# Attention into a SwiGLU block: when the pieces of V are loaded, and when one copy is queued

## Chip, core and metric

The kernel runs on one core of a Trainium2 chip. The metric is the device time of one execution in microseconds, of which several runs are given. An execution under the hardware profiler gives the trace that is read here. The engines are TensorE (PE; its weight loads are a row of their own, PEld), VectorE (DVE), ScalarE (ACT), GpSimd (POOL) and SyncE (SP), which issues most of the transfers.

## What is computed

For 8 batches of 8 heads, 576 positions and head dimension 64: causal attention whose scores get a bias from a running sum of max(s, 0), then a gated feed-forward block over all 4608 tokens.

```
scores = scale * q @ k.T;  cum = cumsum(max(s, 0))
scores = where(causal, -1e9, scores + min(-(cum_i - cum_j), 0))
attn = softmax(scores);  x = (attn @ v), heads side by side     # 4608 x 512
g = x @ w_gate;  out = (g * sigmoid(g) * (x @ w_val)) @ w_out
```

## The kernel before

**Attention.** The 64 pairs of batch and head are worked in 16 half-batches of 4 heads. In the code `h` is the half-batch, `step` its head (0 to 3) and `ci` one of the four pieces of a head's score matrix (`score_piece`, L352). Half-batches 2b and 2b+1 are batch b; I call h "even" or "odd". A score piece is one to four matmuls (L373) from the operand tile `kq` into a PSUM bank, and one ACT activation (L383) that takes the exponential and frees the bank. The weighted sum with V (`av_piece`, L410) is followed by a DVE reciprocal and multiplication (`av_out`, L426 and L427), which free its bank. There are 8 banks; `take` gives out the one that was freed longest ago.

**Feed-forward.** `ffn_items(tt)` yields the work of tile tt (512 tokens) in small items: for each of 12 column blocks a gate product G and a value product V (`gate_value`, matmuls at L643), then the output product (L700 for tiles 0 and 1, L749 after). A gate product is followed by ACT's tanh (`th`, L664) and DVE's `pp` (L666), which frees its bank; a value product by DVE's `ht` (L677). The products read `XT`, the transposed attention output, one 128-row part per matmul.

**The order** is written out by hand: after each feed-forward item the loop pumps `attn_items` up to a given position, and each score piece calls `side` (L481) and `side_v` (L531), which hold tables of what else is issued there. Every engine works through its own instructions in that order. SP has one queue; an SP instruction that waits holds up all that follow.

**How k and q come in.** For half-batch hb: `load_qk` brings both from memory (rawk, rawq, 576 KB each); a cast makes them bf16 (ck, cq); `scratch` (L272) writes them to memory (ks, qs, 288 KB each); `transposes` (L281) reads them back transposed into pk and pq, single buffers; `split` (L286) is four DVE copies from pk and pq to `kq`. I write "ks 8" or "pk 8" for those of half-batch 8. Splits are not issued at once: `side` puts them into the list `later`, and `do_later(1)` takes one out at fixed feed-forward items (in tile 1 after every second item), `do_later(4)` the rest before the next transposes and at the start of a half-batch.

**How V comes in.** V of batch bn is five pieces of up to 128 positions (256 KB, the last 128 KB), each a transfer of its own on SP (`load_v`, L156) into `rawv`, which is a single buffer, and a cast into `vt` (`cast_v`, L167) on ACT for batch 3 and later (L171). V of batch bn is loaded in half-batch 2(bn-1) and cast in 2(bn-1)+1: batch 3 in half-batches 4 and 5, batch 4 in 6 and 7. A cast waits for its own piece alone. I write "V 3 piece 2".

**How x goes out.** For each pair of heads from batch 2 on, POOL writes the output to memory (`x_out`, xs) and SP reads it back transposed into `XT` (`x_in`, L451, after odd steps), in one or two parts.

Of the kernel before, what the change touches and what calls it, by code (L numbers as in the profile page):

```python
# [19 lines left out]
def kernel(  # L20
# [11 lines left out]
    nc = tc.nc  # L32
    PSUM = bass.MemoryType.PSUM

    B, H, S, D = q.shape
# [68 lines left out]
    first = first_sbuf.enter_context(tc.tile_pool(name="first", bufs=1))  # L104
# [9 lines left out]
    with tc.manual_schedule():  # L114
# [37 lines left out]
        def load_qk(hb):  # L152
            load_one(hb, "k")
            load_one(hb, "q")

        def load_v(b, cs, eng=nc.sync):  # L156
            if 0 in cs:
                loaded["v", b] = raw.tile([128, NCH, H, D], FP32, tag="rawv", bufs=1, name="rawv")
            t = loaded["v", b]
            for c in cs:  # L160
                n = 128 if c < 4 else TAIL
                eng.dma_start(
                    t[0:n, c, :, :],
                    v[b, :, c * 128 : c * 128 + n, :].rearrange("h p d -> p h d"),
                )

        def cast_v(b, c, eng):  # L167
            n = 128 if c < 4 else TAIL
            dst, src_t = VT[b % 2][0:n, c, :, 0:D], loaded["v", b][0:n, c, :, :]
            if eng is nc.scalar:  # L170
                nc.scalar.copy(dst, src_t)  # L171
            else:
                eng.tensor_copy(dst, src_t)  # L173
# [9 lines left out]
        def aug(hb, engs, hhs=range(HB)):  # L183
            for hh in hhs:
                r, e = divmod(hh, 2)
                r0 = 64 * (1 - r)
                bh = hb * HB + hh
                engs[hh].dma_start(  # L188
                    KQ[hb % 2][r][r0 : r0 + 4, :, e * S : (e + 1) * S],
                    HL[bh : bh + 1, :, :, :],  # L190
                )
# [61 lines left out]
        def cast_one(hb, name, eng):  # L253
            cts[name, hb] = cp.tile([128, J, NR, D], BF16, tag="c" + name, bufs=2, name="c" + name)
            dst = cts[name, hb].rearrange("x j r d -> x r j d")
            src_t = loaded[name, hb]
            if eng is nc.scalar:
                nc.scalar.copy(dst, src_t)
            else:
                eng.tensor_copy(dst, src_t)  # L260
# [11 lines left out]
        def scratch(hb):  # L272
            for name, SC in (("k", KS), ("q", QS)):
                nc.sync.dma_start(
                    SC[hb].rearrange("(x j) c -> x (j c)", j=J),
                    cts[name, hb].rearrange("x j r d -> x (j r d)"),
                )
# [3 lines left out]
        def transposes(hb):  # L281
            for name, SC in (("k", KS), ("q", QS)):
                prs[name, hb] = cp.tile([128, NR * S], BF16, tag="p" + name, bufs=1, name="p" + name)
                nc.sync.dma_start_transpose(prs[name, hb], SC[hb])
# [186 lines left out]
        def do_later(n):  # L471
            while n > 0 and later:
                f, *args = later.pop(0)
                f(*args)
                n -= 1
# [5 lines left out]
        def side(h, step, ci):  # L481
            bh = HB * h + step
            for c in V1_AT.get((bh, ci), ()):
                cast_v(1, c, nc.gpsimd)
            if bh == H + 4 and ci == 3:
                load_v(2, range(5))
            if h == 4 and (step, ci) in ((0, 1), (2, 1)):
                load_qk(6 + step // 2)
            if h >= 5 and h + 3 < NHB and (step, ci) == (0, 1):
                load_qk(h + 3)  # L490
            hb = h + 1
            if NPE <= hb < NHB:
                late = hb == NPE
                if late and (step, ci) == (0, 1):
                    scratch(hb)
                if late and (step, ci) == (0, 3):
                    transposes(hb)
                if (step, ci) == (0, 1):
                    aug(hb, GP4)
                first = 1 if hb < NPE + 3 else 0  # L500
                if step in (first, first + 1) and ci == (3 if late else 1):
                    for r in range(NR):
                        later.append((split, hb, "kq"[step - first], r))
            hb = h + 2
            if hb == NPE and step == 3 and ci % 2 == 1:
                cast_one(hb, "kq"[ci // 2], nc.gpsimd)
            if NPE < hb < NHB:
                six = hb == NPE + 1
                if (step, ci) == ((2, 0) if six else (0, 2)):
                    cast_one(hb, "k", nc.scalar)  # L510
                if (step, ci) == ((2, 2) if six else (1, 2)):
                    cast_one(hb, "q", nc.scalar)
                if (step, ci) == ((3, 0) if six else (2, 0)):
                    scratch(hb)
                if (step, ci) == (3, 3 if six else 0):
                    do_later(NR * 2)
                    transposes(hb)
            if ci != 1:
                return
            bn = h // 2 + 1  # L520
            if 3 <= bn < B:
                if h % 2 == 0:
                    if step == 2:
                        load_v(bn, (0, 1))
                    if step == 3:
                        load_v(bn, (2, 3, 4))

        V2_AT = {(1, 0): 0, (1, 1): 1, (1, 2): 2, (1, 3): 3, (2, 0): 4}
        V_AT = {(1, 0): 0, (2, 0): 1, (2, 2): 2, (3, 0): 3, (3, 2): 4}

        def side_v(h, step, ci):  # L531
            bn = h // 2 + 1
            if h == 4 and (step, ci) in V2_AT:
                cast_v(2, V2_AT[step, ci], nc.gpsimd)
            if 3 <= bn < B and h % 2 == 1 and (step, ci) in V_AT:
                cast_v(bn, V_AT[step, ci], nc.scalar)

        seconds = []

# [21 lines left out]
        def attn_items():  # L561
            for kk in range(H, BH + 2):
                h, step = divmod(kk, HB)
                if kk < BH:
                    if step == 0:
                        do_later(NR * 2)
                    if step == 1 and 3 < h + 1 < NPE:
                        cast_one(h + 1, "k", nc.gpsimd)
                        cast_one(h + 1, "q", nc.gpsimd)
                    if step == 2 and 3 < h + 1 < NPE:  # L570
                        aug(h + 1, GP4)
                    for ci in range(4):
                        score_piece(kk, ci)
                        side(h, step, ci)
                        side_v(h, step, ci)
                        yield kk + 0.1 + ci / 8
                        if (step, ci) in PREP_AT.get(h, ()):
                            prep_one(
                                h + 1, PREP_AT[h][step, ci],
                                (nc.scalar, nc.vector)[ci // 2] if h == 2 else None,  # L580
                            )
                            yield kk + 0.1 + ci / 8
# [327 lines left out]
        def pick(side):  # L910
            b = PICK[side]
            for lo in range(2):
                for c0, c1 in ((0, 512), (512, S)):
                    nc.tensor.matmul(
                        banks[:, b + c0 // 512, 0 : c1 - c0], sel[:, lo, :],
                        HL[:, lo, 1, c0:c1], start=(lo == 0), stop=(lo == 1),
                        skip_group_check=True,
                    )

        def picked_row(side):  # L920
            b = PICK[side]
            src_t = banks.rearrange("p b n -> p (b n)")[up, b * 512 : b * 512 + S]
            dst = KQ[0][0][up, side, 0:S]
            if side == 1:
                nc.scalar.activation(
                    dst, src_t, AF.Identity, bias=r_m[up, 0:1], scale=r_k[up, 0:1]
                )
            else:
                nc.vector.tensor_scalar(
                    dst, src_t, r_q[up, :], r_k[up, :], ALU.mult, ALU.add  # L930
                )
            give(b)
            give(b + 1)
# [102 lines left out]
        at = attn_items()  # L1036
# [84 lines left out]
```

## Time and profile before

| | |
|---|---|
| runs | 374.61 us median, 373.37 to 375.18 (3 runs) |
| the profiled execution | 373.92 us; its span 371.97 us, so 1.95 us lie outside the span |
| clock granted to PE | 0.998 of full speed |
| busy | PE 363.2, DVE 291.1, ACT 239.9, POOL 212.4 us |
| moved by DMA | 64.21 MB, most of it on SP's queue (41.46 MB) |

"Busy" is the union of an engine's instructions. Matmuls overlap, and their ends are modelled: one of 512 columns is shown with 0.379 us, but in an unbroken row each starts 0.216 us after the one before (four in 0.86 us), one of 65 columns 0.029 us. So I count what PE loses from start to start. In a timeline row the bracket is the engine's idle time before it and what ended it. When a transfer has landed is read from the trace's record of semaphore updates: each transfer of this kernel's queues makes 16, and I take the last.

### The profile page before, as it was taken

How to read it: one execution, taken by the hardware profiler on the slowest of the kernel's cores; microseconds unless marked ns; L12 is line 12 of the kernel's file. 1: busy time of each engine (PE TensorE's matmuls, PEld its weight loads, DVE VectorE, ACT ScalarE, POOL GpSimd, SP SyncE). 2: the span in 40 equal slices, each digit the busy share in tenths (PEclk: the TensorE clock that was granted, in tenths of full speed). 3: DMA queues.
4: the chain of work that ended last, by engine and by line, in shares of the span. 5: the costliest groups of instructions: out<-in, count | busy, mean ns of one | idle time of the engine just before them, and what ended most of it. 6: DMA issues, size and time to landing. Idle time of an engine off the chain costs nothing.

```text
span 372.0 us, 8786 instructions
## 1 busy us (share of the span) xinstructions
PE 363.2 (98%) x3288; PEld 230.3 (62%) x3288; DVE 291.1 (78%) x585; ACT 239.9 (65%) x470; POOL 212.4 (57%) x325
## 2 busy tenths in 40 slices
PE   7899999999999999999999999999999999999996
PEld 6684556655555557855685558655865585476465
DVE  8978776377985899589967897699868867975984
ACT  8877776778886967688757875786565523323321
POOL 8983556955266547594749464955675516315320
PEclk9999999999999999999999999999999999999999
DMA  7999999799879996996789484994142113002003
GB/s 238 220 254 259 215 272 257 239 299 227 252 172 307 199 268 181 162 285 217 214 179 263 160 185 157 265 210 114 40 121 62 35 30 118 0 3 86 28 0 113
DMA packets 97133, 64.21 MB, mean 173 GB/s; under 512 B 77228, under 2 KB 82724, under 8 KB 97092
## 3 DMA queue, kind: packets, MB, share of 16 engines
q1 hardware_dynamic: 84964, 41.46, 46.9%
q0 software_dynamic: 12128, 22.21, 22.7%
q8 instruction: 25, 0.41, 0.5%
q14 instruction: 16, 0.13, 0.1%
HBM read 37.90 MB, written 19.86 MB: 155 GB/s over the span
## 4 chain that ended last, share of the span: by engine, by line
PE 83%; DVE 10%; DMA 2%; ACT 2%; issue 2%; POOL 1%; DVEq 0%; ACTq 0%
PE banks L643 43%; PE banks L749 17%; PE banks L373 9%; PE banks L410 7%; PE banks L700 5%; DVE kq L330 3%; DMA pk<-ks 2%; DVE pp L666 2%; DVE ht L677 1%; DVE kq L288 1%; ACT th L664 1%; POOL vt L173 1%; ACT pt L383 1%; PE banks L459 1%; PE banks L301 0%
## 5 line engine op out<-in xcount | busy, mean ns | idle before, releaser
L383 ACT ACTIVATE pt<-banks 128x512 bf16<-128x512 f32 (+1 forms) x256 | 120.4, 511 | 29.8 <-PE banks L373 17.1
L643 PE MATMUL banks<-XT,wg 128*128 128x512 bf16 x432 | 111.4, 379 | 0.4 <-DVE pp L666 0.3
L643 PE MATMUL banks<-XT,wv 128*128 128x512 bf16 x432 | 110.9, 379 | 0.1
L664 ACT ACTIVATE th<-banks 128x512 bf16<-128x512 f32 x108 | 64.7, 599 | 56.3 <-PE banks L643 51.4
L666 DVE SCALAR_TENSOR_TENSOR pp<-th,banks 128x512 bf16<-128x512 bf16 x108 | 73.7, 682 | 18.3 <-ACT th L664 18.0
L677 DVE SCALAR_TENSOR_TENSOR ht<-pp,banks 128x512 bf16<-128x512 bf16 x108 | 74.1, 687 | 10.3
L373 PE MATMUL banks<-kq 128*128 128x128 bf16 (+4 forms) x576 | 76.4, 240 | 0.8 <-DVE kq L330 0.3
L686 POOL TENSOR_TENSOR ht<-ht 128x512 bf16<-128x512 bf16 x35 | 40.4, 1154 | 53.3 <-DVE su L684 53.2
L373 PEld LDWEIGHTS <-kq 128*128 128x128 bf16 x576 | 46.1, 98 | 30.7 <-issue 2.4
L643 PEld LDWEIGHTS <-wv 128*128 128x128 bf16 x432 | 38.4, 98 | 36.2 <-issue 0.2
L643 PEld LDWEIGHTS <-wg 128*128 128x128 bf16 x432 | 38.4, 98 | 34.1 <-issue 0.7
L410 PEld LDWEIGHTS <-pt 128*128 128x128 bf16 x960 | 41.8, 98 | 17.7 <-issue 0.7
L388 POOL TENSOR_SCALAR_AFFINE_SELECT pt<-pt 128x512 bf16<-128x512 bf16 x56 | 36.6, 653 | 25.9 <-ACT pt L383 21.7
L410 PE MATMUL banks<-vt,pt 128*128 128x65 bf16 x960 | 46.8, 194 | 0.5 <-DVE ot L427 0.4
L444 POOL DMA_DIRECT2D xs<-ot x24 | 21.7, 904 | 30.4 <-DVE ot L427 28.0
L749 PEld LDWEIGHTS <-ht 128*128 128x128 bf16 x336 | 31.2, 98 | 4.3
L427 DVE TENSOR_TENSOR ot<-banks,rc 128x320 bf16<-128x320 f32 x64 | 31.5, 492 | 2.2
L188 POOL DMA_DIRECT2D kq<-HL x48 | 29.2, 610 | 0.0
L700 PE MATMUL banks<-wo,ht 128*128 128x512 bf16 x96 | 25.8, 379 | 0.0
L749 PEld LDWEIGHTS <-su 128*128 128x128 bf16 x252 | 23.6, 98 | 3.3
L814 POOL TENSOR_TENSOR ysb<-ysb 128x512 f32<-128x512 f32 x12 | 15.2, 1269 | 15.3 <-DVE ysb L808 15.3
L749 PE MATMUL banks<-WS,ht 128*128 128x256 bf16 x168 | 22.9, 273 | 0.0
(101 smaller groups left out, 377.2 us busy)
## 6 DMA issues: line engine op xcount, KB each, us to landing
out_dram<-ysb POOLq DMA_DIRECT2D x32, 256.0 KB, 4.0
rawv<-in_v_dram SPq DMA_DIRECT2D x28, 256.0 KB
rawk<-in_k_dram SPq DMA_DIRECT2D x12, 576.0 KB
rawq<-in_q_dram SPq DMA_DIRECT2D x12, 576.0 KB
xs<-ot POOLq DMA_DIRECT2D x24, 160.0 KB, 3.7
ks<-ck SPq DMA_DIRECT2D x11, 288.0 KB
qs<-cq SPq DMA_DIRECT2D x11, 288.0 KB
rawk<-in_k_dram POOLq DMA_DIRECT2D x3, 576.0 KB, 6.0
```

The source lines that it names most:

```text
L373: nc.tensor.matmul(sc[:, o : o + w], T[:, 1, e * S + 128 * tj : e * S + 128 * (tj + 1)], T[:, 0, e * S + lo : e * S + hi], start=not maske ...
L383: nc.scalar.activation(pt[:, c0 : c0 + n], sc, AF.Exp, scale=0.125)
L388: nc.gpsimd.affine_select(pt[:, 1088:1600], pt[:, 1088:1600], pattern=[[0, 4], [1, 128]], compare_op=ALU.is_ge, fill=zreg, base=0, channel ...
L410: nc.tensor.matmul(av[:, bi * (D + 1) : (bi + 1) * (D + 1)], pt[:, c0 : c0 + 128], VT[b % 2][:, tj, h, :], start=(tj == 0), stop=(tj == bi),)
L427: nc.vector.tensor_mul(ot[:, :, e * D : (e + 1) * D], av3[:, :, 0:D], rc[:, :, None].to_broadcast([128, NCH, D]),)
L643: nc.tensor.matmul(view(bs, TT), w[:, c, f0 : f0 + 128], xt[:, c, :], start=(c == 0), stop=(c == 3),)
L664: nc.scalar.activation(th, pg, AF.Tanh, scale=0.5)
L666: nc.vector.scalar_tensor_tensor(pp, in0=th, scalar=1.0, in1=pg, op0=ALU.add, op1=ALU.mult)
L677: nc.vector.scalar_tensor_tensor(hp[:, 2 * k2 : 2 * k2 + 2, :].rearrange("p a n -> p (a n)"), in0=pp, scalar=0.5, in1=pv, op0=ALU.mult, op ...
L686: (nc.vector if ft == NFT - 1 else nc.gpsimd).tensor_sub(hp[:, 1:3, :], hp[:, 1:4:2, :], hp[:, 0:3:2, :])
L700: nc.tensor.matmul(view(pys[ts_], DM), hps[ft // 2][:, 2 * (ft % 2) + half, c0 : c0 + 128], WO[j][:, ft % WKO, :], start=(ft == 0), stop=( ...
L749: nc.tensor.matmul(ps, lhs(p), rhs(p), start=(first and p == 0), stop=(last and p == NP - 1), skip_group_check=True,)
```

## The change

In `side` the loads of V get tables of their own, one piece at an entry. An entry is (0 for an even half-batch or 1 for an odd one, step, ci).

```
-                if step in (first, first + 1) and ci == (3 if late else 1):
+                if step in (first, first + 1) and ci == (3 if late and step == first else 1):
                     for r in range(NR):
                         later.append((split, hb, "kq"[step - first], r))
...
-            if ci != 1:
-                return
-            bn = h // 2 + 1
-            if 3 <= bn < B:
-                if h % 2 == 0:
-                    if step == 2:
-                        load_v(bn, (0, 1))
-                    if step == 3:
-                        load_v(bn, (2, 3, 4))
+            if h >= 4:
+                odd = h % 2
+                at = VLOAD_AT if h > 5 else V3LOAD_AT
+                if h // 2 + 1 < B and (odd, step, ci) in at:
+                    load_v(h // 2 + 1, (at[odd, step, ci],))
+
+        VLOAD_AT = {(0, 0, 3): 0, (0, 1, 0): 1, (1, 0, 0): 2, (1, 0, 3): 3, (1, 1, 0): 4}
+        V3LOAD_AT = {(0, 3, 3): 0, (1, 0, 0): 1, (1, 0, 3): 2, (1, 1, 0): 3, (1, 1, 2): 4}
...
+        V3_AT = {(1, 2): 0, (2, 0): 1, (2, 2): 2, (3, 0): 3, (3, 2): 4}
         V_AT = {(1, 0): 0, (2, 0): 1, (2, 2): 2, (3, 0): 3, (3, 2): 4}
...
+            at = V_AT if bn > 3 else V3_AT
-            if 3 <= bn < B and h % 2 == 1 and (step, ci) in V_AT:
-                cast_v(bn, V_AT[step, ci], nc.scalar)
+            if 3 <= bn < B and h % 2 == 1 and (step, ci) in at:
+                cast_v(bn, at[step, ci], nc.scalar)
```

Before, pieces 0 and 1 were issued at (even, step 2, ci 1) and pieces 2 to 4 at (even, step 3, ci 1). After it, for batch 4 and later, pieces 0 and 1 come at the beginning of the even half-batch and pieces 2 to 4 at the beginning of the odd one. For batch 3, piece 0 comes at the last score piece of half-batch 4, after the transposes of half-batch 6, and pieces 1 to 4 in half-batch 5; the cast of its piece 0 moves from (step 1, ci 0) to (step 1, ci 2). In half-batch 4 the copies of q 5 are put into `later` at (step 2, ci 1), before at (step 2, ci 3). No transfer, cast or copy is added or taken away.

## Prediction

> **What bounds the kernel now.** I read the busy totals first, then the busy time in stretches of 10 us, then the timeline where PE loses time.
>
> ```profile
> PE 363.2 (98%) x3288; PEld 230.3 (62%) x3288; DVE 291.1 (78%) x585; ACT 239.9 (65%) x470; POOL 212.4 (57%) x325
> ```
>
> PE sets the time. The stretches show 10.00 us of PE in every ten from 60 to 360 us except two, the first and the last here (the first number after the stretch is its length, then PE, PEld, DVE, ACT, POOL, each with its count).
>
> ```profile
> 80.00:90.00 10.00, 9.74 (x86) 5.52 (x84) 8.42 (x17) 7.58 (x16) 5.03 (x9) 1.00 0.99 267
> ...
> 130.00:140.00 10.00, 9.60 (x84) 5.29 (x82) 9.33 (x20) 7.01 (x16) 4.85 (x8) 1.00 0.89 260
> ```
>
> The change begins at half-batch 4 (67 us), so these two stalls are all it can win. The timeline has both.
>
> ```profile
> 82.25 0.95 DVE L288 COPY kq<-pq 64x1152 bf16<-64x1152 bf16 x1
> ...
> 83.34 0.38 PE L373 MATMUL banks<-kq 128*128 128x128 bf16 x4 [0.26 <-DVE kq L288]
> ```
>
> Stall 1: the matmuls before it are nine of 65 columns from 82.65; at 0.029 each their turn ends at 82.91; PE goes on at 83.34: 0.43 us, for the first copy of q 5.
>
> ```profile
> 125.62 0.84 DVE L288 COPY kq<-pk 64x1152 bf16<-64x1152 bf16 x1 [0.76 <-DMA pk<-ks]
> ...
> 130.01 1.03 PE L643 MATMUL banks<-XT,wg 128*128 128x512 bf16 x4
> ...
> 131.44 0.47 PE L410 MATMUL banks<-vt,pt 128*128 128x65 bf16 x10 [0.40 <-DVE ot L427]
> ```
>
> Stall 2: four matmuls from 130.01 at 0.216 end at 130.87; PE goes on at 131.44: 0.57 us. It waits for the multiplication of the head before (DVE, 130.90 to 131.39), and DVE has gone without a pause worth the name since 125.62, where it had stood 0.76 us for pk 8. So the ceiling of a gain is 0.43 + 0.57 = 1.00 us.
>
> **Copies of q 5: nothing.** Queued later or sooner, they leave `later` at its slots. In tile 1 these come after the value products, every second item: the first takes the first k copy (77.44), the next the second (79.30), the third the first q copy (82.25). By the loops, q entered the list at half-batch 4 step 2 ci 3, between the first slot and the second; ci 1 lies there too. The list gives the k copies first, so every copy keeps its place on DVE, and stall 1 stays. A gain would need an earlier slot; that is excluded. 0.00.
>
> **pk 8 sooner: -0.57.** Its chain on SP:
>
> ```profile
> 108.94 2.45 SPq L451 DMA_TRANSPOSE XT<-xs  x2
> 111.50 0.53 SPq L274 DMA_DIRECT2D ks<-ck  x1
> 112.12 0.38 SPq L274 DMA_DIRECT2D qs<-cq  x1
> 112.55 1.81 SPq L162 DMA_DIRECT2D rawv<-in_v_dram  x2
> 118.37 2.59 SPq L284 DMA_TRANSPOSE pk<-ks  x1
> ```
>
> ks 8 lands at 118.32, then the transpose is issued and lands 7.22 us later (125.59), behind V 4 pieces 0 and 1 (120.44, 121.74). pk 7 and pk 9, with no V between, took 4.05 and 4.15. The change puts the two pieces ahead of the x transposes (108.94) and of ks 8. They cost the queue 2 x 0.9 to 1.3 us (between the landings of pieces 0 and 1: V 3 0.92, V 4 1.30), say 2.3. Against that SP comes sooner to this place: k 9, the transfer ahead of it, was issued at 107.81, 5.26 us of transposes after ks 7 had landed (102.55). ks 7 can gain from nothing to 1.9 us (k 9 needs the x output that landed at 103.38, and two x transposes of 1.25 after it: 105.9); I take 0.7, nearer to nothing, since V 3 is now ahead of it. So ks 8 lands at 118.32 + 2.3 - 0.7 = 119.9 and pk 8 4.15 later, 124.1. DVE is ready for it at 125.62 - 0.76 = 124.86. The wait goes, and stall 2 with it: -0.57; ends -0.57 (nothing else waits there) and 0 (pk 8 lands at 125.6 again).
>
> **V 3 against its casts: +1.0.** Here something new may be late. Before, all of V 3 had landed at 91.24. Now SP goes: ks 6 directly behind q 7 (landed 83.54), landing about 84.3 where it was 86.42; pk 6 84.3, pq 6 85.6 (by their 1.18 and 1.42), piece 0 87.0, the x transposes 87.6 (2.55), piece 1 90.2, k 8 90.9, q 8 91.5, pieces 2, 3, 4 at 92.0, 92.6, 93.2. k 8 took 4.16 us to land, q 8 1.51 more: 95.1 and 96.6. A piece is 0.8 to 0.9 behind the one before: piece 2 at 97.4, 3 at 98.3, 4 at 98.8. The casts stand here (before, nothing waited):
>
> ```profile
> 95.45 0.64 ACT L171 CAST vt<-rawv 128x512 bf16<-128x512 f32 x1
> ...
> 96.37 0.60 ACT L664 ACTIVATE th<-banks 128x512 bf16<-128x512 f32 x1 [0.17 <-PE banks L643]
> ...
> 97.22 0.67 DVE L666 SCALAR_TENSOR_TENSOR pp<-th,banks 128x512 bf16<-128x512 bf16 x1
> ...
> 98.68 1.03 PE L643 MATMUL banks<-XT,wv 128*128 128x512 bf16 x4
> ```
>
> The first is the cast of piece 2. ACT works in order: behind a waiting cast stand the exponentials and this tanh, behind the tanh DVE's pp, which frees the bank that PE takes at 98.68. A delay d of the cast ends the tanh at 96.97 + d, pp 0.73 later at 97.70 + d; with 0.05 to hand over, PE stands d - 0.93. With d = 97.4 - 95.45 = 1.95: 1.0 us, which a full PE never gets back. Ends: 0 (piece 2 by 96.4) and 2.4 (two us later than I think: the slowest of a transfer's 16 updates came 1.7 after the others at q 7 and at ks 7). Pieces 0 (landing 91, cast now near 92.0) and 1 (94.1 against 93.50) cost nothing beyond that; 3 and 4 come in the shadow of 2. The 0.96 us that DVE stood for pk 6 at 92.67 go too, but PE lost nothing by them.
>
> All of this takes it that a transfer waits for those ahead of it on SP's queue: the 118 SP transfers issued from 60 to 262 us landed in the order of issue, every one.
>
> [...]
>
> **x of batch 2: 0.** The last matmul of tile 2's first gate product needs the x transpose issued at 108.94; it landed at 116.31 and was used at 117.05. The two V 4 pieces now go ahead: 116.31 + 2.3 - 0.7 = 117.9, and the need moves by the 1.0 above to 118.05. Ends 0 and 1.6 (SP no sooner, V 3 in time: 118.6 - 117.05).
>
> **Batch 4 on otherwise: 0.** After pk 8 (119.9), pq 8 (121.2) and one x transpose (122.6), SP issues V 4 piece 2 at 124.0, k 10 and q 10 at 124.6 and 125.2, pieces 3 and 4 by 126.4. Piece 2 lands 4 us later, 128, against its cast at 130.68; k 10 and q 10 by 130.8 (q 10 took 6.54 behind three pieces of V; 5.6 with one ahead), pieces 3 and 4 by 132.5, against 133.72 and 136.09. Later batches have more room: V 5's pieces 2 to 4 go out around k 12, which was issued at 163.89 after them and landed with q 12 by 170.88; without the pieces ahead of pk 10 (issue 2.28 and 2.72 us, else 1.2 and 1.4) that is some 3 us sooner, so they land by about 168, against casts at 170.30, 172.79 and 175.16. Pieces 0 and 1 fall where SP stood idle (142 to 149). PE loses nothing there now, so nothing can be won.
>
> **Sum.** -0.57 + 1.0 = +0.43 on 373.92 (span 371.97 + 1.95): 374.35. The median of the runs is 0.69 above the profiled execution: 375.0.
>
> **Rivals.** (a) Everything in time: pieces 2 and on land by 96.4, pk 8 by 124.9: -0.57, 374.0. For it: DMA moved 49 GB/s at 94, there is room; against it: 1.15 MB of k 8 and q 8 stand ahead. (b) The x transpose is the late one, V 3 in time: +1.6, stall 2 gone in its shade, since DVE's work moves with PE: net +1.1, 375.7. (c) Slower, on the side I don't forecast: the queue of V 3 at the casts. From a landing of piece 2 at 98.9 (d = 3.45, 2.5 - 0.57 = +1.9) the loss is over 0.5%; at 99.4 it is 3.0 - 0.57 = +2.4, 377.0. For it: 7 to 8 us from issue to landing happened here (V 3 before, 7.4 and 7.9); against it: those stood behind k 7, q 7 and two output stores at once, and this stretch has no stores. (d) The change doesn't do what it says: true of the q 5 copies, by the list; that is in the forecast.
>
> **Chances.** Forecast 0.45, (a) 0.27, (b) 0.10, (c) 0.15, something else gaining over 0.5% 0.03. 0.5% (1.87 us) is about what a measurement of this kernel tells from no change. Faster 0.03, slower 0.17, the rest 0.80. Range: from (a) less 0.6 for the spread of the runs, 373.4, to 376.7, between (b) and (c).
>
> **What would show it.** Stall 1 as before, 0.43; no DVE wait for pk 8 or pk 6; pk 8 landing near 124; an ACT wait of 1 to 2 us before the cast of V 3 piece 2 and a PE stall near 99. If ACT does not wait there, (a) holds; if PE stands at tile 2's first gate product, (b); if stall 1 goes, my reading of the list is wrong.

## The result, and the profile after

| | before | after |
|---|---|---|
| median of 6 runs each, side by side | 374.26 us (373.35 to 375.66) | 379.37 us (376.77 to 380.99) |
| the profiled execution, its span | 373.92 us, 371.97 | 379.21 us, 377.3 |

The ratio of the means is 1.0127, with a 95% interval of 1.0082 to 1.0172. The change costs 1.3%, about 5 us, and lies above the predicted range. Below, the times are medians of all executions, while a ratio leaves out an execution that is more than 1.5% above the fastest of its kernel (one each of e1_v3_only, e2_v4_only and e8_v4_four_ahead). (In the changed file the lines behind the tables are one higher: L643 is L644, L664 is L665, L666 is L667; in some of the experiments L643 is L645 or L647.)

Where PE loses it is told first by its waits. The view gives the line, what it waited for, the total, how often, and the longest.

```profile
PE banks L644 <- DMA XT<-xs: 2.0, 1, 2.0
PE banks L644 <- DVE pp L667: 1.4, 2, 1.0
PE banks L373 <- ACT pt L383: 0.7, 1, 0.7
PE banks L373 <- DVE kq L288: 0.3, 1, 0.3
```

The first three lines have no large counterpart in the kernel before; the last is stall 1, unchanged. The stretches of 10 us (length, then PE, PEld, DVE, ACT, POOL, the granted clock, the DMA share, GB/s) place them:

```profile
80.00:90.00 10.00, 9.74 (x85) 5.53 (x84) 8.42 (x17) 7.31 (x15) 5.04 (x9) 1.00 0.78 184
90.00:100.00 10.00, 9.00 (x80) 4.96 (x78) 6.51 (x13) 6.87 (x15) 2.68 (x5) 1.00 0.86 236
100.00:110.00 10.00, 9.30 (x86) 5.34 (x86) 9.62 (x19) 9.01 (x18) 6.51 (x11) 1.00 0.72 162
110.00:120.00 10.00, 9.23 (x81) 5.06 (x79) 6.17 (x12) 6.18 (x13) 5.00 (x10) 1.00 1.13 253
120.00:130.00 10.00, 8.76 (x63) 4.48 (x63) 5.69 (x13) 5.08 (x10) 4.68 (x8) 0.83 1.03 245
130.00:140.00 10.00, 10.00 (x85) 5.51 (x84) 9.13 (x18) 8.95 (x18) 4.92 (x7) 1.00 0.79 208
```

80 to 90 is as before. 130 to 140 is full now: stall 2 has gone. From 90 to 130 PE loses in two places, and from 120 to 130 the clock column has 0.83: a part of it (122.48 to 125.90 us) ran at half clock, 0.50. The timeline of PE at these places:

```profile
83.33 0.38 PE L373 MATMUL banks<-kq 128*128 128x128 bf16 x4 [0.26 <-DVE kq L288]
...
99.49 0.19 PE L373 MATMUL banks<-kq 128*128 128x64 bf16 x1 [0.68 <-ACT pt L383]
100.70 1.02 PE L644 MATMUL banks<-XT,wv 128*128 128x512 bf16 x4 [1.02 <-DVE pp L667]
...
121.24 0.38 PE L644 MATMUL banks<-XT,wg 128*128 128x512 bf16 x1 [2.01 <-DMA XT<-xs]
...
123.12 1.91 PE L644 MATMUL banks<-XT,wg 128*128 128x512 bf16 x4
```

Counted from start to start, PE loses 0.85 + 1.18 = 2.03 us at 99 to 101 and 2.17 us before 121.24. The last row is no wait: four matmuls of 512 columns, 1.03 us elsewhere, take 1.91 at half clock.

**The first loss** comes from ACT, which stands for a piece of V 3:

```profile
94.48 1.08 ACT L383 ACTIVATE pt<-banks 128x512 bf16<-128x512 f32 x2
98.70 0.62 ACT L171 CAST vt<-rawv 128x512 bf16<-128x512 f32 x1 [3.13 <-DMA rawv<-in_v_dram]
...
99.34 0.59 ACT L665 ACTIVATE th<-banks 128x512 bf16<-128x512 f32 x1
```

That is the cast of piece 2, which stood at 95.45 before. Behind it are the exponentials that PE's first wait names, and the tanh that must come before the pp of the second. **The second loss** is tile 2's first gate product, waiting for the x transpose of pair 11 (the last pair of heads of batch 2). Before, its four matmuls ran without a wait:

```profile
116.41 1.02 PE L643 MATMUL banks<-XT,wg 128*128 128x512 bf16 x4
```

Both losses go back to SP's queue (start, time in issue; after the change):

```profile
90.34 0.47 SPq L145 DMA_DIRECT2D rawq<-in_q_dram  x1
90.86 6.96 SPq L162 DMA_DIRECT2D rawv<-in_v_dram  x3
97.98 2.46 SPq L451 DMA_TRANSPOSE XT<-xs  x2
...
109.97 0.57 SPq L145 DMA_DIRECT2D rawk<-in_k_dram  x1
110.59 0.47 SPq L145 DMA_DIRECT2D rawq<-in_q_dram  x1
111.11 1.29 SPq L162 DMA_DIRECT2D rawv<-in_v_dram  x2
112.50 5.68 SPq L451 DMA_TRANSPOSE XT<-xs  x2
```

k 8 landed at 94.26 and q 8 only at 97.79, 7.44 us after its issue; V 3's pieces 2, 3 and 4 followed at 98.67, 100.01 and 100.31. The issue of piece 4 alone held SP from 92.89 to 97.82, until q 8 was in. The x transposes behind it wait for an output of x that POOL writes, issued at 90.60; it took 7.36 us to land (97.96), where before it took 3.42. So two things kept these transposes until 97.98: the held issue and this write. So all that follows on SP is late, k 9 among it: issued at 109.97, landed at 114.50, where before it was 107.81 and 112.35. Behind k 9 now stand q 9 and V 4's pieces 0 and 1 (landed 117.84 and 120.03), and then pair 11's x transpose, 121.20, where it was 116.31.

The sum for this execution: 2.03 + 2.17 + 1.7 (3.41 us at half clock) - 0.57 (stall 2) = 5.33, against 377.3 - 371.97 = 5.3 in span. Two later profiles of the same kernel have the first loss again, but half of the second and no half clock behind it (next section), so this sum is not that of every execution.

### The profile page after: what moved, and what is told of

It reads as the page before. It is cut to its first block, busy times and chain, and to the rows that moved or that the text cites. A ratio compares the mean times of both kernels' runs of the same rounds, so it can differ in the third digit from the quotient of the medians.

```text
span 377.3 us, 8795 instructions
## 1 busy us (share of the span) xinstructions
PE 365.5 (97%) x3288; PEld 231.4 (61%) x3288; DVE 291.6 (77%) x585; ACT 240.1 (64%) x470; POOL 212.3 (56%) x325
## 4 chain that ended last, share of the span: by engine, by line
PE 84%; DVE 7%; DMA 3%; ACT 2%; issue 1%; SPq 1%; POOL 1%; DVEq 0%; ACTq 0%
PE banks L644 45%; PE banks L750 17%; PE banks L373 9%; PE banks L410 7%; PE banks L701 4%; DVE kq L330 3%; DMA XT<-xs 2%; DVE pp L667 2%; DVE ht L678 1%; DMA rawk<-in_k_dram 1%; PE banks L315 1%; POOL vt L173 1%; ACT pt L383 1%; ACT th L665 1%; PE banks L459 1%
## 5 line engine op out<-in xcount | busy, mean ns | idle before, releaser
L644 PE MATMUL banks<-XT,wg 128*128 128x512 bf16 x432 | 112.4, 381 | 2.4 <-DMA XT<-xs 2.0
L644 PE MATMUL banks<-XT,wv 128*128 128x512 bf16 x432 | 111.3, 380 | 1.1 <-DVE pp L667 1.0
L665 ACT ACTIVATE th<-banks 128x512 bf16<-128x512 f32 x108 | 64.6, 598 | 59.1 <-PE banks L644 55.4
L667 DVE SCALAR_TENSOR_TENSOR pp<-th,banks 128x512 bf16<-128x512 bf16 x108 | 73.6, 682 | 25.1 <-ACT th L665 24.7
L644 PEld LDWEIGHTS <-wv 128*128 128x128 bf16 x432 | 38.6, 98 | 38.3 <-issue 2.4
L644 PEld LDWEIGHTS <-wg 128*128 128x128 bf16 x432 | 38.6, 98 | 34.7 <-issue 1.7
L393 POOL TENSOR_SCALAR_AFFINE_SELECT pt<-pt 128x64 bf16<-128x64 bf16 x56 | 14.7, 263 | 18.1 <-ACT pt L383 18.0
```

The source lines that it names most:

```text
L644: nc.tensor.matmul(view(bs, TT), w[:, c, f0 : f0 + 128], xt[:, c, :], start=(c == 0), stop=(c == 3),)
L665: nc.scalar.activation(th, pg, AF.Tanh, scale=0.5)
L667: nc.vector.scalar_tensor_tensor(pp, in0=th, scalar=1.0, in1=pg, op0=ALU.add, op1=ALU.mult)
```

## The experiments

All kernels were made from the changed file; where the expectation says "the kernel before with one edit", the edit for q 5 is still in, but DVE's order of work is the same with it and without it. Only the tables of loads differ (V3LOAD_AT for batch 3, V4LOAD_AT for batch 4, VLOAD_AT for the rest; an entry may name several pieces). OLD stands for the slots before, `{(0, 2, 1): (0, 1), (0, 3, 1): (2, 3, 4)}`, NEW3 and NEW for those of the change.

First the losses in the profiled execution of each, in us from start to start (the three of the change are after, after_again and after_third, the four of V 3 alone e1_v3_only to e1_fourth), since the medians mix in what varies between executions. "Start" is how much later than 83.34 stall 1 stands, which only the first 60 us can cause. "Sum" adds the row without the column of stall 2, and subtracts 0.57 where that stall is gone (in e1_fourth it is there as before, with 0.58); beside it what the span differs from 371.97.

| kernel | start | V 3's casts | pair 11's x | half clock behind a stall | stall 2 | near 250 | sum | span differs |
|---|---|---|---|---|---|---|---|---|
| after | 0.0 | 2.03 | 2.17 | 1.7 | gone | 0 | 5.3 | 5.3 |
| after_again | 0.0 | 2.03 | 1.01 | 0 | gone | 0.51 | 3.0 | 2.9 |
| after_third | 3.83 | 2.05 | 1.08 | 0 | gone | 0 | 6.4 | 6.4 |
| e1_v3_only | 0.33 | 2.09 | 0 | 0 | gone | 0 | 1.9 | 1.8 |
| e1_again | 0.0 | 1.87 | 0 | 0 | gone | 0 | 1.3 | 1.2 |
| e1_third | 0.0 | 1.89 | 0 | 0 | gone | 0 | 1.3 | 1.3 |
| e1_fourth | 0.24 | 2.69 | 0 | 1.7 | 0.58 | 0.57 | 5.2 | 5.1 |
| e2_v4_only | 0.75 | 0 | 1.13 | 0 | gone | 0 | 1.3 | 1.3 |
| e3_v5on_only | 2.03 | 0 | 0 | 0 | gone | 1.24 | 2.7 | 2.7 |
| e4_v3_ahead_k8 | 2.81 | 0 | 1.70 | 0 | gone | 0 | 3.9 | 3.9 |
| e5_v4_behind | 0.0 | 0 | 0 | 0 | gone | 0 | -0.5 | -0.6 |
| e7_v4_one_ahead | 0.14 | 0 | 0 | 0 | gone | 0 | -0.4 | -0.5 |
| e8_v4_four_ahead | 1.08 | 0 | 1.23 | 0 | gone | 0 | 1.7 | 1.8 |
| e9_v3_casts_late | 0.0 | 0 | 4.39 | 1.5 | gone | 1.22 | 6.5 | 6.4 |
| e10_both_mended | 0.0 | 0 | 0 | 0 | gone | 0.50 | -0.1 | -0.1 |

(e6_q5_early has no stall from 60 us on; without stall 1 its start can't be read so. Its span is 371.0.) The sums close to 0.1 us, so these columns hold all that the profiled executions lost.

### The change in three parts

**e1_v3_only**: V 3 and the cast of its piece 0 as in the change.

```
V3LOAD_AT = NEW3;  V4LOAD_AT = OLD;  VLOAD_AT = OLD
```

> Only V 3 as in the change; V 4 and later as before. Theory (three separate costs: the casts of V 3 wait for pieces behind k 8 and q 8, 2.03 us; the x transpose of pair 11 stands behind V 4 pieces 0 and 1, 2.17 us; half clock for 3.41 us after the second stall, 1.7 us; less the 0.57 of the old stall): PE stands 2.0 us near 100, nothing near 119, clock 1.0; the old stall of 0.57 may stay. Time 376.3 to 376.9 against 374.3 before. Rival (V 3 alone sets off everything, since SP is held up by it and all that follows comes late): also a stall of 2 us near 120 and the half clock, 379 as in the changed kernel.

Measured: 378.61 us, ratio 1.0096 (1.0067 to 1.0125), between the theory's 376.9 and the rival's 379. The profile (375.86 us) is as the theory had it: 2.09 us at the casts, nothing at the x transpose; the median has more, see the last group of experiments. **e2_v4_only**: V 4 alone.

```
V3LOAD_AT = OLD (cast as before);  V4LOAD_AT = NEW;  VLOAD_AT = OLD
```

> Only V 4 as in the change; V 3, V 5 and later as before. Theory: no wait near 100; pair 11's x lands near 119.0 to 119.5 against a need at 117.3: PE stands 1.7 to 2.2 us there, perhaps with half clock after it (1.7 us); the old stall of 0.57 goes. Time 375.4 to 377.4. Rival (V 3 alone sets off everything): no stall, 373.7 to 374.3.

Measured: 376.73 us, ratio 1.0039 (1.0011 to 1.0067). PE waits at the x transpose, 1.13 us from start to start, less than the 1.7 to 2.2 of the theory:

```profile
118.93 0.38 PE L645 MATMUL banks<-XT,wg 128*128 128x512 bf16 x1 [0.96 <-DMA XT<-xs]
```

**e3_v5on_only**: V 5 and later.

```
V3LOAD_AT = OLD (cast as before);  V4LOAD_AT = OLD;  VLOAD_AT = NEW
```

> Only V 5 to V 7 as in the change; V 3 and V 4 as before. Theory: no PE stall but the two old ones, 374.3 as before. Rival (the early pieces of the later batches cost something too): a stall after 140, over 374.9.

Measured: 374.88 us, ratio 1.0011 (0.9987 to 1.0035): no difference that can be told. So V 3's place costs most, V 4's some, and the rest hardly anything in the median. But e3's profiled execution does lose 1.24 us near 250, and DVE shows why:

```profile
245.80 0.54 DVE L288 COPY kq<-pk 64x1152 bf16<-64x1152 bf16 x1 [1.73 <-DMA pk<-ks]
```

That is pk 14. V 7's pieces 0 and 1, issued at 223.88 and 224.39, stand ahead of an output of x that POOL writes at 225.56; this landed after 7.25 us instead of 4.32, the x transpose that waits for it went out at 232.83 instead of 228.42 (PE had started 2.03 later here), and with it ks 14 and pk 14, which had only 0.4 us of room before (landed 242.09, copied at 242.52). In the seven profiled executions with V 5 on moved that output took 5.95 to 7.25 us to land, in the ten without it 3.08 to 4.81. PE lost 0.5 to 1.2 us near 250 in four of the seven (e3, e9, e10, after_again), and 0.57 in one of the ten (e1_fourth), so the moved pieces make it likelier and are not all of its cause.

### V 3 ahead of k 8

**e4_v3_ahead_k8**: the change, but V 3's pieces 1 to 4 go out together, ahead of k 8 and q 8.

```
V3LOAD_AT = {(0, 3, 3): (0,), (1, 0, 0): (1, 2, 3, 4)};  V4LOAD_AT = NEW;  VLOAD_AT = NEW
```

> The change with V 3 pieces 1 to 4 all ahead of k 8 and q 8. Theory: the pieces land before their casts, no stall near 100; SP isn't held up in V 3 piece 4 and reaches k 9 near 106.5 instead of 110.3; pair 11's x lands 11.2 us after k 9 is issued, 117.7 against 117.3: stall 0 to 1 us, no half clock, the old 0.57 gone. Time 374.0 to 375.0. Rival (V 4 pieces 0 and 1 ahead of pair 11's x cost over 2 us wherever SP stands): stall of 2 us and half clock, 376 to 378.

Measured: 377.86 us, ratio 1.0079 (1.0053 to 1.0106), nearer to the rival. The wait at the casts is gone, so it was k 8 and q 8 standing ahead of the pieces. But the x transpose is now 1.70 us late:

```profile
110.58 0.57 SPq L145 DMA_DIRECT2D rawk<-in_k_dram  x1
121.56 0.38 PE L645 MATMUL banks<-XT,wg 128*128 128x512 bf16 x1 [1.54 <-DMA XT<-xs]
```

k 9 is not to blame here. In this execution PE started 2.81 us later; counted from there k 9 went out at 107.77, as before (107.81). So V 3 ahead of k 8 does free SP, and what is left is V 4's two pieces, 6.60 us from the landing of k 9 to that of the x transpose, where it was 3.96 before. Counted in the same way, k 9 went out at 108.7 to 110.2 in the eight traces with V 3 placed as in the change, and at 105.1 to 108.2 in eight of the nine others (e6's start is not known).

### The x transpose and the number of pieces ahead of it

**e7_v4_one_ahead**: one piece of V 4 ahead of pair 11's x transposes.

```
V3LOAD_AT = OLD;  VLOAD_AT = OLD;  V4LOAD_AT = {(0, 0, 3): (0,), (0, 3, 1): (1, 2, 3, 4)}
V4_AT = {(1, 0): 0, (2, 2): 1, (3, 0): 2, (3, 2): 3, (3, 3): 4}      # casts of V 4
```

> The kernel before with one piece of V 4, not two, ahead of pair 11's x transposes (half-batch 6 step 0 ci 3), the other four behind the transposes of k and q 8. Theory (each piece puts the x transpose back by the 0.9 to 1.3 us that it costs the queue; it had 0.74 us of room): PE stands 0.2 to 0.6 us at tile 2's first gate product instead of the 1.13 with two pieces, the stall at 131 is gone: -0.57 + 0.4 = about -0.2 against before at an equal clock. Rival (the x transpose is late because SP is held in issuing, whatever the count): as with two pieces, 1.1 us or more.

Measured: 373.49 us, in one execution; the x transpose landed at 116.89 and PE did not stand. **e8_v4_four_ahead**: four pieces ahead.

```
V3LOAD_AT = OLD;  VLOAD_AT = OLD;  V4LOAD_AT = {(0, 0, 3): (0, 1, 2, 3), (0, 3, 1): (4,)}
```

> The kernel before with four pieces of V 4 ahead of pair 11's x transposes (half-batch 6 step 0 ci 3), the fifth behind the transposes of k and q 8; V 3 and V 5 on as before. Theory: the x transpose lands 4 x 0.9 to 1.3 = 3.6 to 5.2 us later, PE stands 2.9 to 4.5 us in one piece at tile 2's first gate product, and, as behind the 2.17 us stall of the changed kernel, the granted clock falls to half for about 3.4 us right after it, 1.7 us more: in all +4.0 to +5.6 with stall 2 gone, 378 to 380, and the mean granted clock of nearly every execution 0.995 or less. Rival (the half clock in the changed kernel was chance, as the one at the start of another run): the stall alone, no half clock behind it, clock 1.0 in most executions, +2.3 to +3.9, 376.5 to 378.5.

Measured: 378.66 us, ratio 1.0142 (1.0078 to 1.0205), in the theory's range; but the profiled execution (375.82 us) lost only 1.23 us at the x transpose, which fits neither:

```profile
119.36 0.38 PE L645 MATMUL banks<-XT,wg 128*128 128x512 bf16 x1 [1.07 <-DMA XT<-xs]
```

The landings tell what was wrong with the expectation. From the landing of k 9 to that of the x transpose it is 3.96 us with no piece between (before; 2.8 to 3.3 in e3, e10 and three times in e1; 5.4 to 5.8 in e5, e6 and e1_fourth, where SP came to the transpose only after a wait), 5.76 with one (e7), 7.30 with two (e2), 6.70 with two (after), 8.71 with four (e8): against 3.96, 1.2 to 1.8 us a piece, against 2.8 to 3.3 up to 2.9. But k 9 itself landed at 112.35 (before), 111.13 (e7), 111.58 (e2), 114.50 (after) and 110.62 (e8). When k 9 lands moves by 1.7 us between executions even where nothing ahead of it was changed (before, e7, e2, e8), and PE's start by 1.08 in e8. The other three executions of e8 had a mean granted clock of 0.995, 0.995 and 0.987, so they ran in part below the full clock; where, is not recorded, and the median's agreement with the theory shows nothing of its mechanism. So the room of the x transpose is no fixed 0.74 us, and a piece ahead of it costs something in some executions and nothing in others.

### Does the second loss wait behind the first?

**e9_v3_casts_late**: the change with later casts of V 3, so that none waits.

```
-        V3_AT = {(1, 2): 0, (2, 0): 1, (2, 2): 2, (3, 0): 3, (3, 2): 4}
+        V3_AT = {(2, 2): 0, (3, 0): 1, (3, 2): 2, (3, 3): 3}      # piece 4 at h == 6, (0, 1)
```

> The changed kernel with the casts of V 3 later, nothing else: pieces 0 to 3 in half-batch 5 at step 2 ci 2, step 3 ci 0, 2 and 3, piece 4 in half-batch 6 step 0 ci 1, so that each stands behind its landing (piece 2 landed at 98.96, now cast near 99.3). Theory A (the x transpose of pair 11 lands at a time that SP and its queue set, near 121.5, whatever PE does before): the 2.03 us at 99 to 101 go, the need of the x transpose comes 2.0 sooner, and PE stands about 4.2 us there in one piece; nothing is gained by the late casts alone. On the clock: the 3.4 us at half clock lie on a grid of 3.41 us and follow a grid window in which PE was busy 0.41 or less (0.47 and more: none followed); a stall of 4.2 leaves a window at or below 0.41 in nearly any place of the grid, so a half-clock window follows in nearly every execution and the mean clock is 0.995 or less: span near 377.3, time 379. Rival B (the losses simply add): the x stall stays at 2.2, the time falls by 2.0 to 377.

Measured: 380.98 us, ratio 1.0147 (1.0076 to 1.0218); the first loss is gone and the second is 4.39 us in one piece:

```profile
PE banks L647 <- DMA XT<-xs: 4.2, 1, 4.2
```

Theory A holds: the two losses are not to be added as if they were independent. Pair 11's x transpose lands when SP's queue lets it, at 121.37 here and 121.20 in the change, and a stall before it only uses up a part of the same wait.

### Both places mended

**e10_both_mended**: V 3 ahead of k 8, V 4 behind the transposes of k and q 8, V 5 on as in the change.

```
V3LOAD_AT = {(0, 3, 3): (0,), (1, 0, 0): (1, 2, 3, 4)};  V4LOAD_AT = {(0, 3, 1): (0, 1, 2, 3, 4)}
V4_AT = {(2, 0): 0, (2, 2): 1, (3, 0): 2, (3, 2): 3, (3, 3): 4};  VLOAD_AT = NEW
```

> The changed kernel with its two places mended: V 3's pieces 1 to 4 ahead of k 8 and q 8, and all of V 4 behind the transposes of k and q 8 with later casts; V 5 on as in the change. Theory (the loss is the order on SP at these two places, and k 9 going out 2.4 to 2.8 us later than before costs nothing without V 4 ahead of the x transpose: it would land near 118.8 against a need of 117.3): no stall at 99 to 101; at the x transpose 0 to 1.5 us remain, since without the V 3 stall its need comes 2 us sooner; stall 2 gone; at 250 to 255 between 0 and 1.2 us from V 7's first pieces. Between -0.6 and +1.5 against before, a median of 374.2 to 376.1. Rival (the late SP alone makes the x transpose late by 2 us or more, V 4 is innocent): above 376.5.

Measured: 375.3 us, ratio 1.0024 (1.0001 to 1.0048); the interval just leaves out 1. No stall at the casts, none at the x transpose (landed 115.47, before the 118.8 that was expected), and 0.50 us near 250. What is left of the change's 1.3% is 0.2%. So the two places are the cause of nearly all of it. The later k 9 is not an independent third: in this profile it went out at 108.17, against 107.81 before.

### Stall 2 and stall 1 taken away

**e5_v4_behind**: all of V 4 behind pk 8 and pq 8, casts as in e10; V 3 and V 5 on as before.

```
V3LOAD_AT = OLD;  VLOAD_AT = OLD;  V4LOAD_AT = {(0, 3, 1): (0, 1, 2, 3, 4)}
```

> The kernel before with one edit: all five pieces of V 4 are issued behind the transposes of k and q 8, and four of their casts stand one slot later (the first in half-batch 7 step 2, the last in step 3, its last slot). V 3 and V 5 on as in the kernel before. Theory (a transfer on SP's queue lands behind those ahead of it, each piece of V 0.9 to 1.3 us; PE's loss is the landing less the need, and nothing else): pk 8 lands near 123 and DVE does not wait for it, the stall at 131.4 goes (-0.57), pair 11's x transpose lands as before and costs nothing, the pieces of V 4 land by 131 against casts from 128.6 to 137: 0.57 less, a median near 374.0, a ratio of 0.9985, within what can be told from 1. Rival: the pieces push batch 3's x transposes and k 10 and q 10 back by 2.5 us and one of them becomes the late one, 0 to +2 us, 374.5 to 376.5.

Measured: 374.4 us beside 374.93, ratio 0.9976 (0.9947 to 1.0005). pk 8 is copied without a wait, and the stretch with stall 2 is full:

```profile
124.81 0.96 DVE L288 COPY kq<-pk 64x1152 bf16<-64x1152 bf16 x1
```

```profile
130.00:140.00 10.00, 10.00 (x86) 5.57 (x85) 9.35 (x21) 8.10 (x18) 4.88 (x7) 1.00 1.02 250
```

**e6_q5_early**: the same, and a copy of q 5 that is really sooner.

```
+            if h == 4 and (step, ci) == (3, 0):
+                do_later(1)
```

> The edit of the run with V 4 behind the transposes, and one copy of q 5 that is really sooner: the list of copies is served once more at half-batch 4 step 3 ci 0, so that on DVE the first q 5 copy stands before the multiplication that ends a value product and not behind it, and the second before the addition of tanh that follows. Theory (stall 1 is PE waiting for this copy alone): the 0.43 us at 83.3 go as well, 0.43 + 0.57 = 1.0 less than before, a median near 373.6, a ratio of 0.997. Rival (DVE is the bound there: the copies push the multiplication 0.9 and the addition 0.5 us back, and these free banks): the stall stays in another place, 0 to 0.4 us at 83 to 86, and the median is that of the other run, near 374.0.

Measured: 374.08 us beside 374.93, ratio 0.9981 (0.9954 to 1.0007). The nine matmuls from 82.63 now run straight into the scores, where stall 1 stood:

```profile
82.63 0.43 PE L410 MATMUL banks<-vt,pt 128*128 128x65 bf16 x9
82.90 0.39 PE L373 MATMUL banks<-kq 128*128 128x128 bf16 x4
```

Its span, 371.0, is 1.0 below before, the whole ceiling of 0.43 + 0.57. The profiled spans of e6 and e5 lie 1.0 and 0.6 us below that of the kernel before; by the medians neither can be told from it, since both intervals hold 1.

### The change again, and V 3 alone again

> The changed kernel, one more look. Theory: the same two stalls (2.0 us at 99 to 101, 1.9 to 2.4 at 119 to 122), and a half-clock window only if a window of the 3.41 us grid holds 2.0 us or more of a stall: 377.3 in span with it, about 375.5 without. Rival: the half clock comes somewhere else, without a stall.

> As the look before: the same two stalls at the same places to within 0.3 us; with a half-clock window the span is 377.3, without about 375.5.

The same two stalls at the same places; the second was 1.01 and 1.08, not 1.9 to 2.4, with no half clock behind it. after_third has a half-clock window, but at 15.8 us, in the start, after a window in which PE was busy 1.28 us of 3.41: the rival's case, and no part of the change.

> V 3 as in the change, the rest as before: one more look, for the 2 us by which most of its executions were longer than the profiled one (span 373.8; the others 375.5 to 376.6 at full clock). Theory: where the start is alike, pair 11's x transpose is late in these by 1 to 2 us, since k 9 goes out 2.8 us later than before and the room was 0.74 plus the 2.09 that the V 3 stall gives; or the stall at the casts is longer, 3 us. Rival: the two stalls are as in the profiled run and the difference lies in the first 60 us.

> V 3 as in the change, the rest as before. Its two looks so far lost 1.9 to 2.1 us at 97 to 101 and nothing after, spans 373.2 and 373.8, yet most of its other executions were longer, 375.5 to 376.6 at full clock. Theory: in some executions pair 11's x transpose or pk 8 comes late as well, or the stall at the casts is 3 us and more; then this look may show a span above 375 with that stall in it. Rival: the executions without a profile differ in the first 60 us.

> As the look before: a span of 373.2 to 373.8 with 1.9 to 2.1 us lost at 97 to 101, or one above 375 with a further stall that this look then places.

The first two repeat 373.2 and 373.3 in span. The last is a long one, 377.1, and shows what can happen in those: the casts cost 2.69 (piece 2 landed at 99.58), a half-clock window follows, pk 8 lands at 130.56 and stall 2 is back, and pk 14 is late. So V 3's place, less stall 2, costs 1.3 to 1.5 us in three of the four profiled executions, and 2.69 + 1.7 = 4.4 in the one whose stall is a little longer (the 0.57 near 250 comes on top). That is a way to a median 4 us up; how often it happens in the executions without a profile can't be read, so the median of V 3 alone is explained only in part.

## Why the prediction was wrong, point by point

**Stall 1 stays, the q 5 copies do nothing: right.** 0.42 us at 83.33, and DVE's order unchanged. e6 shows that the ceiling was real and a sooner slot would have had it.

**pk 8 sooner, -0.57: right in size, in the change by luck.** No DVE wait for pk 8, no PE stall near 131. The landing was to be 124.1 and was 126.73, but DVE, held up with PE, came to the copy at 130.45, 5.6 us later, which made the room. e2, with V 4 alone placed as in the change, is the better test: pk 8 landed at 123.77 and was copied without a wait at 126.65. In e5, with nothing held up, it landed at 124.45 and was copied at 124.81.

**V 3 against its casts, +1.0: the mechanism was right, the size was not: 2.03.** I put q 8 at 1.51 us behind k 8, by the row of q 8 before, behind which only transposes stood. In the change it was 3.53 (2.0 to 2.9 in its other executions and those of e1). That V's pieces behind it are the reason is not shown: in e9, with the same pieces, it was 1.70 (k 8 had taken longer), in e5, with none, 2.50. "This stretch has no stores" overlooked POOL's write of x at 90.6, which was under way at the same time and landed 7.36 us later. Piece 2 landed 0.88 behind q 8, as taken: at 98.67, not 97.4. By my own formula, d - 0.93, the cast at 98.70 gives 2.3. My upper end, 2.4, held the 2.03, and the rival (c) had its landing (98.9).

**x of batch 2, 0: this step failed, 2.17 (1.0 to 1.1 in the other two executions).** "Against that SP comes sooner to this place" was wrong in sign: k 9 landed 2.15 later than before (0.8 and 0.9 in the other two, counted from PE's start), not 0.7 earlier. I had reckoned each issue on SP at its own 0.5 to 1.3 us, and had not asked whether an issue could stand while earlier transfers were under way. The issue of V 3's last piece took 4.93 us. The trace of the kernel before has six such issues, of 2.6 to 4.5 us, the first that of V 3's piece 1 at 77.29 (3.13 us, with k 7, q 7 and piece 0 not yet in), so it could have been read there. The cost of V 4's two pieces was 2.74, near the 2.3 that I took. Together: 2.15 + 2.74 = 4.89 later, less the 0.74 of room and the 2.02 by which the need moved, gives 2.13, against 2.17. My upper end for this term, 1.6 with SP no sooner and V 3 in time, is nearly what e4 has, 1.70.

**The rivals were taken apart where they belong together.** (b) asks for "V 3 in time" and (c) for a late V 3 with the x transpose in time. Both go back to the same queue: what holds V 3 holds SP, and so k 9, and so the x transpose. Their joint case, 2.03 + 2.17 - 0.57 = +3.6 even without the half clock, stood in no chance and in no range. (The net of (b) itself was added up wrongly: 1.6 - 0.57 is 1.0, not 1.1.)

**The half clock, 1.7 in the profiled execution: not in the prediction at all.** I priced a stall at its own length. See the last section.

**Batch 4 on, 0: nearly.** Pieces 2 to 4 land in time. But with V 7's first pieces ahead of it POOL's write of x took 7.25 us to land in e3, where it took 4.32 before, and in four of the seven profiled executions with V 5 on moved PE loses 0.5 to 1.2 us near 250. I looked at where the pieces fall on SP, and not at POOL's transfers, which were under way at the same time; e3's ratio, 1.0011, says that it is little in the median.

**"A transfer waits for those ahead of it on SP's queue": held.** The 117 SP transfers issued between 60 and 262 us in the trace of the change landed in the order of issue, every one. In the other 16 traces it was the same, with 116 to 118 transfers each.

## What to carry to other kernels

When a load is moved on a queue, follow the issuing engine too: with earlier transfers under way the issue of V 3's last piece stood for 4.93 us here, and k 9, 17 us further on, still started 2.2 us late. Rivals that go back to one queue can come true together; price them as one case and let the range reach it. And move a load behind what is needed soon, not ahead: in the profiles of e5 and e7, with most or all of V 4 behind the transposes, stall 2 is gone and no new stall stands. Last, compare two executions from the same point of the work: k 9 of e4 looked 2.8 us late only because PE had started 2.8 us later.

## What the hardware did that I had not expected

**The 2.17 us stall of the change had half clock behind it, 1.7 us more.** In the trace of the change the granted clock is 0.50 from 122.48 to 125.90 us, for 3.41 us, and again from 378.48, 75 such lengths after the first. In the trace before it is 0.50 from 370.53, 107 such lengths after its first record of the clock at 5.31. I read each trace along such a grid of 3.41 us (length, PE busy, and the clock behind POOL's column). The change, then e1_fourth, then e9, then e3 at its start:

```profile
119.07:122.48 3.41, 1.40 (x18) 0.88 (x17) 0.79 (x3) 0.77 (x2) 1.28 (x3) 1.00 0.96 225
122.48:125.90 3.42, 3.42 (x12) 1.38 (x10) 2.41 (x6) 1.15 (x3) 2.99 (x5) 0.50 0.98 279
```

```profile
99.13:102.54 3.41, 1.12 (x8) 0.55 (x8) 1.61 (x4) 2.93 (x7) 0.30 (x2) 1.00 0.58 150
102.54:105.96 3.42, 3.42 (x26) 2.01 (x25) 2.81 (x7) 2.08 (x6) 1.66 (x3) 0.50 1.01 195
```

```profile
117.53:120.95 3.42, 0.00 (x0) 0.00 (x0) 0.15 (x1) 0.00 (x0) 0.78 (x2) 1.00 1.10 290
120.95:124.36 3.41, 2.94 (x18) 1.63 (x18) 1.28 (x3) 1.19 (x2) 0.68 (x2) 0.50 0.66 230
```

```profile
11.99:15.40 3.41, 1.26 (x15) 1.05 (x16) 3.07 (x5) 1.21 (x4) 2.51 (x4) 1.00 1.03 236
15.40:18.81 3.41, 3.41 (x27) 2.62 (x25) 3.04 (x5) 2.52 (x6) 3.29 (x7) 0.50 0.83 108
```

In these four the half-clock window follows one in which PE was busy 1.40, 1.12, 0.00 and 1.26 us. Two windows that were a little busier, 1.59 and 1.96, have full clock behind them: e1_v3_only and e4.

```profile
97.76:101.17 3.41, 1.59 (x10) 0.80 (x10) 0.79 (x2) 2.06 (x5) 0.24 (x1) 1.00 0.56 122
101.17:104.59 3.42, 3.42 (x33) 1.91 (x33) 3.19 (x7) 3.27 (x8) 1.73 (x3) 1.00 0.68 222
```

```profile
120.11:123.52 3.41, 1.96 (x20) 1.17 (x20) 1.23 (x4) 1.08 (x2) 1.37 (x3) 1.00 0.86 311
123.52:126.94 3.42, 3.37 (x32) 1.94 (x32) 3.21 (x7) 2.74 (x6) 2.67 (x5) 1.00 1.07 220
```

In these traces all five windows of 1.40 us or less inside the work (0.00, 1.12, 1.26, 1.28 in after_third, 1.40) were followed by half clock, and none of 1.59 or more was. The end of each trace, where PE runs out of work, agrees: a last window with 1.22 us (before) has half clock behind it, one with 1.55 (e10) has not. In the change PE was not busy for 2.01 us of the window ahead of the half clock (3.41 - 1.40). The grid does not stand at the same place in every execution (5.3 us in before, 6.4 in the change, from the start of the span), so how much of a stall falls into one window differs too. That can be a good part of why the change's times spread over 4 us, which is my estimate: its two executions with a mean granted clock of 1.0 took 376.77 and 377.21 us, the four with 0.994 to 0.995 took 379.21 to 380.99; where in those without a profile the half clock stood is not recorded. The rows show what followed what in these traces; what sets the clock they do not show, and PE's busy share was not varied by itself.

**Two issues on SP stood for over 4 us, with earlier transfers under way.** The issue of a transfer, 0.4 to 1.3 us mostly in the trace of the change, took 4.93 us at 92.89 (until 97.82, q 8 landed at 97.79), and the x transpose's 4.40 at 112.50 (until 116.90, q 9 landed at 116.09). It is no wait for the data of the instruction itself: the semaphores that the two wait for had their last update at 89.58 and at 111.08. In these two places k, q and two pieces of V were outstanding, and the next issue ended 0.03 and 0.81 us after q was in. In e8 it was the third piece (3.39 us, until 112.01, q 9 landed at 112.23). In the kernel before, V 4's pieces 0 and 1 went out in 0.48 and 1.28 us (112.55 and 113.08) with q 9, two x transposes, ks 8 and qs 8 not yet in. So no rule can be read from these rows; which count or size matters was not tried.
